# A list of work up to chunk 3 ordered anew: block-diagonal states, k and q by SyncE, v by converting transfers of GpSimd

## The chip, the cores and the metric

The kernel runs on one core of one Trainium2 chip. A core has TensorE (PE, with its weight loads shown as PEld), VectorE (DVE), ScalarE (ACT), GpSimd (POOL) and SyncE (SP, which here only issues DMAs), and 16 DMA engines that all queues share. The metric is the time of one launch on the device, in microseconds; lower is better. The kernel before takes 214.64 us, the median of 3 runs (214.52 to 214.77).

## What is computed

Attention with a decay per head, block by block with a running state, and then a feed-forward layer on the attention's output. The sizes: 4 batches, 8 heads, 768 positions, 64 wide; 3072 tokens of 512, hidden width 2048. Inputs and output are float32; the kernel multiplies in float16.

```python
def _attn_ref(q, k, v, lam):                  # q, k, v: (4, 8, 768, 64)
    ...
    for b in range(nb):                       # blocks of 64 positions
        intra = einsum('bhic,bhjc->bhij', qb, kb) * Dmask[None]
        intra = einsum('bhij,bhjd->bhid', intra, vb)
        inter = einsum('bhid,bhde->bhie', qb * lam_pow[None], kv_state)
        out[:, :, sl] = intra + inter
        kb_dec = kb * rev_pow[None]
        kv_state = lam_block[None, :, None, None] * kv_state + einsum('bhsd,bhse->bhde', kb_dec, vb)
    return out

def _moe_ref(x, w_in, w_out, alpha):          # x: (3072, 512)
    h = x @ w_in                              # (3072, 2048)
    g = maximum(h, 0.0) + alpha * minimum(h, 0.0)
    return g @ w_out
```

## The kernel before

The work is cut into 6 chunks. A chunk is 256 positions (two blocks of 128) of two batches, 512 tokens, so a chunk of the feed-forward has the full width of a matmul. Chunks 0 and 1 are the first 256 positions of batches 0, 1 and of 2, 3; chunks 2 and 3 the next 256, and so on. Each chunk has four units: one batch, one half of the heads. There are 24 units, numbered in order; unit 4c to 4c+3 belong to chunk c, and the halves of one batch are neighbours.

A unit needs k, q and v. `load` (L79) brings a half of the heads of one of them, 256 KB of float32, over SyncE's queue, in pieces of 512 bytes; with `None` it brings both halves. `cast` (L257) makes float16 of them on ScalarE ("A"), VectorE ("V") or GpSimd ("G"). `load_v16` (L268) is in the kernel, but nothing calls it before: a DMA on GpSimd's queue that reads v as float32 and writes it as float16 straight into the unit's v16 tile, so that neither a raw tile nor a cast is needed. `key_decayed` (L281) multiplies k by its decay. k and q are transposed by TensorE and copied back, both at once (`transposes`, L298, with "D" instead a transposing DMA of SyncE) or one of them (`transposed`, L324). `decayed` (L342) multiplies the transposed q by its decay.

The products of a unit are `score_products` and `masked` (L376, L391), `intra` (L401), `inter` (L360, which reads the state R of the block before) and `state_products` (L421), from which `states` (L448) makes the next R. `attended` (L437) writes the result, transposed already, to xT of the chunk. `cluster(old, new)` (L471) puts the second half of one unit's products and the first half of another's side by side in one accumulator bank; `scores` and `state` (L487, L491) do the scores and the state of one unit without it, and `state` first clears two banks with a matmul against zeros each (L495).

The feed-forward of a chunk is 16 times `up` (L503: four matmuls, the activation on ScalarE L516 and VectorE L525; with `bi` 0 or 1 only one batch's half of the width), and for four groups of 128 tokens four `down` steps of four matmuls (L532), whose last stores the result. `fill` (L133) issues matmuls whose result nothing reads.

The weights come in four groups each of 512 KB float16: `load_win` (L94) and `load_wout` (L106), converting DMAs on GpSimd's queue. `gate` (L114) is a tiny DMA on SyncE's queue that reads one element of a weight group; it can start only once that group has landed, and SyncE's later loads wait behind it.

All engines run their instructions in the order in which the program issues them. For chunks 0 to 2 and the loads of chunk 4 this order is a list written out by hand (L609 to L919); chunks 3 to 5 are woven by a loop (L921 to L929), and the last down-projections follow (L930). Buffers come round: five sets of raw tiles, four each of the float16 q and k, v16 and kdec tiles, three of the transposed ones, two of masked scores. A tile that is taken again waits until its last reader is done.

Of the kernel before, what the change touches and what calls it, by code (L numbers as in the profile page):

```python
# [11 lines left out]
def kernel(  # L12
# [474 lines left out]
    def scores(n):  # L487
        score_products(n)
        masked(n)
# [116 lines left out]
                a[i]()  # L606
                i += 1

    mask_logs(2)  # L609
    key_decay()  # L610
    load(0, 0, "k", None)
    decay_mask(2)
    query_decay(1, 1)
    cast(1, "k16", "V")
    load(0, 1, "k", 0)
    fill(8, "h")
    mask_logs(1)
    query_decay(2, 1)
    state_decay()
    decay_mask(1)  # L620
    key_decayed(0, "G")
    mask_logs(0)
    load(0, 0, "q", 0)
    cast(0, "k16", "A")
    key_decayed(1, "G")
    load(0, 0, "q", 1)
    query_decay(3, 1)
    decay_mask(0)
    cast(0, "q16", "A")
    load_alpha()  # L630
    cast(2, "k16", "G")
    load(0, 0, "v", 0)
    load(0, 1, "q", None)
    transposed(1, 1, "V", "tk")
    mask_logs(3)
    transposed(0, 1, "A", "h")
    cast(1, "q16", "V")
    transposed(2, 1, "A", "tk")
    decay_mask(3)
    query_decay(0, 1)  # L640
    cast(0, "v16", "A")
    fill(4, "op")
    load(0, 0, "v", 1)
    query_decay(2, 0)
    transposed(1, 0, "V", "h")
    decayed(1, "G")
    transposed(0, 0, "V", "tk")
    slopes()
    cluster(None, 0, "A")
    cast(2, "q16", "V")  # L650
    decayed(0, "G")
    cast(3, "q16", "A")
    load(0, 1, "v", None)
    load(0, 1, "k", 1)
    fill(4, "tk")
    scores(1)
    cast(1, "v16", "A")
    load(1, 0, "k", 0)
    key_decayed(2, "G")
    load_win(1)  # L660
    cast(3, "v16", "V")
    load_win(0)
    cast(2, "v16", "G")
    state(1, "hh")
    load(1, 0, "q", 0)
    key_decayed(3, "G")
    transposed(2, 0, "A", "tk")
    cluster(0, None, "A")
    cast(3, "k16", "A")
    decayed(2, "P")  # L670
    transposed(3, 0, "A", "op")
    scores(2)
    load_win(2)
    load_win(3)
    cluster(1, None, "A")
    state(2, "hh")
    query_decay(1, 0)
    transposed(3, 1, "A", "op")
    load_wout(1)
    fill(5, "tk")  # L680
    cluster(2, None, "A")
    scores(3)
    decayed(3, "G")
    query_decay(0, 0)
    gate(1, "out")
    load_wout(0)
    load(1, 0, "q", 1)
    state(3, "to")
    cluster(3, None, "V")
    load(1, 0, "v", 0)  # L690
    load_wout(2)
    fill(1, "h")
    up(0, 5, 0, "h")
    up(0, 6, None, "h")
    load(1, 1, "k", 1)
    up(0, 5, 1, "tk")
    cast(4, "k16", "A")
    up(0, 4, None, "h")
    up(0, 7, None, "op")
    up(0, 2, None, "h")  # L700
    load(1, 0, "k", 1)
    load(1, 0, "v", 1)
    cast(5, "q16", "G")
    load(1, 1, "q", 1)
    up(0, 0, None, "h")
    load(1, 1, "v", 1)
    load(1, 1, "k", 0)
    load(1, 1, "q", 0)
    up(0, 3, None, "tk")
    up(0, 10, None, "h")  # L710
    up(0, 9, None, "h")
    up(0, 8, None, "op")
    up(0, 15, None, "tk")
    up(0, 11, None, "h")
    up(0, 12, None, "op")
    load_wout(3)
    load(2, 0, "q", 1)
    load(2, 0, "q", 0)
    load(2, 0, "k", 0)
    cast(4, "q16", "A")  # L720
    up(0, 1, None, "h")
    up(0, 13, None, "h")
    up(0, 14, None, "op")
    transposes(4, "A", False)
    load(1, 1, "v", 0)
    load(2, 0, "k", 1)
    down(0, 2, 0, 4, "h")
    key_decayed(4, "V")
    down(0, 3, 0, 4, "h")
    down(0, 0, 0, 4, "op")  # L730
    down(0, 2, 1, 4, "h")
    cast(4, "v16", "V")
    load(2, 0, "v", 0)
    cast(5, "k16", "V")
    key_decayed(7, "G")
    cast(7, "k16", "A")
    down(0, 0, 1, 4, "op")
    cluster(None, 4, "A")
    transposes(5, "A", False)
    key_decayed(5, "V")  # L740
    decayed(5, "V")
    decayed(4, "G")
    down(0, 3, 1, 4, "h")
    cast(5, "v16", "G")
    down(0, 2, 2, 4, "h")
    cast(7, "q16", "A")
    transposed(7, 1, "V", "tk")
    cluster(4, 5, "A")
    down(0, 3, 2, 4, "h")
    transposed(7, 0, "A", "tk")  # L750
    down(0, 0, 2, 4, "op")
    cast(7, "v16", "A")
    cast(6, "k16", "G")
    cluster(5, 7, "A")
    down(0, 0, 3, 4, "op")
    decayed(7, "V")
    cast(8, "q16", "A")
    cast(6, "q16", "G")
    down(0, 2, 3, 4, "h")
    transposes(6, "V", False)  # L760
    load(2, 1, "v", 1)
    down(0, 1, 0, 4, "op")
    load(2, 1, "k", 0)
    cluster(7, None, "A")
    key_decayed(6, "V")
    load(2, 1, "q", 0)
    cast(8, "k16", "G")
    scores(6)
    down(0, 3, 3, 4, "h")
    cast(6, "v16", "V")  # L770
    cast(9, "q16", "A")
    key_decayed(8, "V")
    transposes(8, "V", False)
    decayed(6, "G")
    load(2, 1, "v", 0)
    down(0, 1, 1, 4, "op")
    cast(8, "v16", "G")
    cast(9, "k16", "A")
    load(2, 0, "v", 1)
    load(3, 0, "k", 0)  # L780
    load(3, 0, "k", 1)
    state(6, "hh")
    decayed(8, "V")
    down(0, 1, 2, 4, "op")
    cluster(6, 8, "A")
    load(2, 1, "k", 1)
    down(0, 1, 3, 4, "op")
    up(1, 2, None, "h")
    up(1, 12, None, "op")
    up(1, 13, None, "h")  # L790
    query_decay(3, 0)
    transposes(9, "V", False)
    up(1, 8, 1, "h")
    cast(10, "k16", "A")
    key_decayed(10, "G")
    up(1, 3, None, "op")
    key_decayed(9, "G")
    cast(10, "q16", "A")
    up(1, 15, None, "h")
    up(1, 4, None, "tk")  # L800
    transposes(10, "D", False)
    cast(9, "v16", "G")
    load(2, 1, "q", 1)
    key_decayed(11, "G")
    cast(10, "v16", "G")
    up(1, 8, 0, "h")
    up(1, 1, None, "op")
    cast(13, "k16", "G")
    up(1, 0, None, "h")
    cast(12, "k16", "G")  # L810
    up(1, 11, None, "tk")
    cluster(None, 9)
    up(1, 6, None, "h")
    up(1, 10, None, "h")
    decayed(9, "G")
    up(1, 7, None, "tk")
    gate(3, "out")
    up(1, 5, None, "op")
    load(3, 0, "q", None)
    cast(11, "k16", "G")  # L820
    cluster(8, 10, "A")
    cast(13, "q16", "V")
    cast(11, "q16", "A")
    decayed(10, "V")
    cast(11, "v16", "G")
    down(1, 0, 0, 4, "h")
    load(3, 0, "v", None)
    transposes(11, "D", False)
    down(1, 1, 0, 4, "h")
    cast(12, "q16", "A")  # L830
    up(1, 14, None, "op")
    down(1, 0, 1, 4, "h")
    up(1, 9, None, "tk")
    transposes(12, "D", False)
    cast(12, "v16", "G")
    key_decayed(12, "G")
    load(3, 1, "v", None)
    cluster(9, None, "A")
    down(1, 1, 1, 4, "h")
    cluster(10, 11, "A")  # L840
    decayed(11, "V")
    load(3, 1, "k", 0)
    key_decayed(13, "G")
    down(1, 1, 2, 4, "h")
    down(1, 0, 2, 4, "h")
    transposes(13, "D", False)
    load(3, 1, "k", 1)
    decayed(12, "V")
    load(3, 1, "q", None)
    down(1, 0, 3, 4, "h")  # L850
    cast(14, "k16", "G")
    cluster(11, 12, "A")
    cast(13, "v16", "A")
    down(1, 1, 3, 4, "h")
    up(2, 0, None, "h")
    load(4, 0, "k", 1)
    up(2, 11, None, "op")
    down(1, 2, 0, 4, "h")
    load(4, 0, "q", None)
    cast(14, "v16", "A")  # L860
    key_decayed(14, "V")
    load(4, 0, "v", 0)
    up(2, 9, None, "tk")
    cluster(12, 13, "V")
    down(1, 2, 1, 4, "h")
    cast(14, "q16", "A")
    up(2, 14, None, "op")
    transposes(14, "D", False)
    down(1, 2, 2, 4, "h")
    decayed(13, "V")  # L870
    load(4, 0, "k", 0)
    cast(15, "k16", "V")
    key_decayed(17, "V")
    down(1, 3, 0, 4, "tk")
    down(1, 2, 3, 4, "h")
    key_decayed(15, "G")
    cast(15, "v16", "A")
    load(4, 0, "v", 1)
    cast(16, "k16", "G")
    cast(17, "k16", "V")  # L880
    up(2, 13, None, "h")
    cast(15, "q16", "V")
    cast(16, "q16", "A")
    cast(17, "q16", "A")
    transposes(15, "D", False)
    down(1, 3, 1, 4, "tk")
    transposes(16, "D", False)
    down(1, 3, 2, 4, "tk")
    down(1, 3, 3, 4, "tk")
    cast(17, "v16", "G")  # L890
    decayed(14, "V")
    up(2, 3, None, "h")
    cluster(13, 14, "A")
    up(2, 6, None, "h")
    load(4, 1, "v", 0)
    up(2, 2, None, "h")
    up(2, 5, None, "op")
    key_decayed(16, "G")
    decayed(15, "G")
    up(2, 10, None, "tk")  # L900
    up(2, 4, None, "h")
    cluster(14, 15, "A")
    up(2, 15, None, "h")
    cast(16, "v16", "G")
    load(4, 1, "q", None)
    up(2, 1, None, "tk")
    load(4, 1, "k", 1)
    load(4, 1, "k", 0)
    up(2, 12, None, "op")
    decayed(16, "G")  # L910
    transposes(17, "D", False)
    up(2, 8, None, "h")
    cast(18, "v16", "G")
    cluster(15, 16, "A")
    key_decayed(18, "G")
    up(2, 7, None, "tk")
    load(4, 1, "v", 1)
    cast(18, "k16", "G")
    cast(18, "q16", "G")  # L919

    for c in range(3, NC):  # L921
        att = []
# [39 lines left out]
```

## Time and profile before

| | before |
| --- | --- |
| median of 3 runs | 214.64 us (214.52 to 214.77) |
| the profiled execution's own time | 214.56 us |
| its span | 212.8 us |
| TensorE busy | 206.7 us, 97% |
| VectorE, ScalarE, GpSimd busy | 138.2, 114.8, 60.2 us |
| HBM read, written | 27.27 MB, 6.29 MB |

The span runs from the first to the last instruction that the profile shows; the rest of the time lies around it. The profile's second part cuts the span into 40 slices of 5.3 us; each digit is the busy share in tenths:

```profile
PE   7799999999999999999999999999999999999994
ACT  7985765466676537366644644644534543444121
POOL 3598002423355411046560094620200000000000
PEclk9999999999999999999999999999999999999999
DMA  6999999999967699999797896044011101110212
```

Its third part shows the DMA queues: packets, MB, and the time that the packets took as a share of the 16 engines' span. q1 is fed by SyncE's loads and stores, q0 by GpSimd's converting transfers.

```profile
q1 hardware_dynamic: 56340, 28.85, 54.2%
q0 software_dynamic: 4224, 4.19, 12.0%
```

A row of the timeline has the start, the length, the engine, the line, the operation and the tiles; xN stands for N instructions in a row, and the bracket tells how long the engine idled before and what released it. A row of the groups has the busy time and the mean duration of one in nanoseconds.

### The profile page before, as it was taken

Reading aid. Unit: us, or ns where it says so; the run is one execution under the profiler, and the core shown is the slowest. Engines: PE = TensorE matmul, PEld = TensorE weight load, DVE = VectorE, ACT = ScalarE, POOL = GpSimd, SP = SyncE. Lnnn points to the kernel's source line nnn. Section 1 sums busy time; section 2 is a strip of 40 time slices with the busy share of each in tenths; the row PEclk is TensorE's granted clock in tenths of the full one; section 3 lists DMA queues with packets and bytes.
Section 4 is the critical chain, followed back from the end, with each engine's and each line's share of the span. In section 5 each row is a group of like instructions: output and inputs, shape, how many; then the busy total and the mean of one; then the engine's idle time right before and its main releaser. Section 6 shows DMA issues by size and latency. Waiting matters only on the chain.

```text
span 212.8 us, 5116 instructions
## 1 busy us (share of the span) xinstructions
PE 206.7 (97%) x2092; PEld 106.5 (50%) x2092; DVE 138.2 (65%) x241; ACT 114.8 (54%) x209; POOL 60.2 (28%) x84
## 2 busy tenths in 40 slices
PE   7799999999999999999999999999999999999994
PEld 2465445655545455455554554554554444444453
DVE  6697787778889987969975565565646344444000
ACT  7985765466676537366644644644534543444121
POOL 3598002423355411046560094620200000000000
PEclk9999999999999999999999999999999999999999
DMA  6999999999967699999797896044011101110212
GB/s 168 290 274 205 207 205 285 207 301 305 294 171 216 106 222 283 235 152 274 175 217 105 219 243 159 0 102 99 7 46 49 40 13 49 51 49 3 99 49 99
DMA packets 60603, 33.37 MB, mean 157 GB/s; under 512 B 16276, under 2 KB 57636, under 8 KB 60580
## 3 DMA queue, kind: packets, MB, share of 16 engines
q1 hardware_dynamic: 56340, 28.85, 54.2%
q0 software_dynamic: 4224, 4.19, 12.0%
q8 instruction: 16, 0.26, 0.5%
q14 instruction: 7, 0.06, 0.1%
q10 hardware_dynamic: 16, 0.00, 0.0%
HBM read 27.27 MB, written 6.29 MB: 158 GB/s over the span
## 4 chain that ended last, share of the span: by engine, by line
PE 96%; DVE 2%; ACT 1%; issue 0%; ACTq 0%; DVEq 0%
PE h_ps L508 39%; PE o_ps L538 33%; PE o_ps L561 7%; PE s L383 4%; PE acc L408 3%; PE unread L140 3%; PE acc L367 2%; PE tp L313 1%; PE acc L428 1%; PE tpx L333 1%; PE unread L138 1%; DVE sm L394 1%; DVE qkT L246 1%; PE kv L495 0%; PE kv L428 0%; DVE dmask L196 0%
## 5 line engine op out<-in xcount | busy, mean ns | idle before, releaser
L525 DVE SCALAR_TENSOR_TENSOR g<-m,oma,h_ps 128x512 f16<-128x512 f32 (+1 forms) x98 | 70.9, 735 | 48.5 <-ACT m L516 46.6
L508 PE MATMUL h_ps<-xT,w_in_sb 128*128 128x512 f16 (+1 forms) x392 | 93.0, 375 | 0.0
L516 ACT ACTIVATE m<-h_ps 128x512 f32<-128x512 f32 (+1 forms) x98 | 57.4, 588 | 57.1 <-PE h_ps L508 56.3
L538 PE MATMUL o_ps<-w_out_sb,g 128*128 128x512 f16 x320 | 80.2, 380 | 0.0
L508 PEld LDWEIGHTS <-w_in_sb 128*128 128x128 f16 x392 | 37.8, 98 | 43.1 <-issue 0.2
L538 PEld LDWEIGHTS <-g 128*128 128x128 f16 x320 | 29.8, 98 | 33.5
L394 DVE TENSOR_TENSOR sm<-s,dmask 128x1024 f16<-128x1024 f32 x24 | 29.3, 1221 | 3.4 <-PE s L383 3.3
L551 ACT ACTIVATE o_sb<-o_ps 128x512 f32<-128x512 f32 (+2 forms) x26 | 14.6, 563 | 20.1 <-PE o_ps L561 10.9
L285 POOL TENSOR_TENSOR kdec<-kraw,kdecay 128x512 f16<-128x512 f32 x18 | 18.9, 1056 | 11.6 <-DMA kraw<-in_k_dram 9.2
L347 POOL TENSOR_TENSOR qdT<-qkT,qdecay 128x512 f16<-128x512 f16 (+1 forms) x15 | 15.2, 1013 | 17.1 <-DMA qkT<-qk 8.1
L244 ACT ACTIVATE xT<-acc 128x512 f16<-128x512 f32 x22 | 13.1, 597 | 10.8 <-PE acc L428 9.1
L458 DVE SCALAR_TENSOR_TENSOR R<-R,rdecay,acc 128x128 f16<-128x128 f16 x56 | 16.1, 342 | 0.1
L248 POOL CAST qk<-kraw 128x512 f16<-128x512 f32 x14 | 8.5, 610 | 24.5 <-DMA kraw<-in_k_dram 11.3
L248 POOL CAST v<-vraw 128x512 f16<-128x512 f32 x15 | 9.4, 629 | 20.1 <-PE h_ps L508 11.5
L561 PE MATMUL o_ps<-w_out_sb,g 128*128 128x512 f16 (+2 forms) x96 | 14.1, 308 | 0.0
L561 PEld LDWEIGHTS <-g 128*128 128x128 f16 x96 | 8.1, 98 | 6.1
L244 ACT ACTIVATE qk<-qraw 128x512 f16<-128x512 f32 x17 | 10.4, 623 | 0.8 <-DMA qraw<-in_q_dram 0.8
L383 PE MATMUL s<-qkT 64*64 64x128 f16 x384 | 10.1, 222 | 0.6 <-DVE qkT L246 0.4
L408 PE MATMUL acc<-sm,v 64*64 64x128 f16 x384 | 9.6, 218 | 0.0
L367 PEld LDWEIGHTS <-R 128*128 128x128 f16 x80 | 6.2, 98 | 5.6 <-ACT R L468 0.6
L367 PE MATMUL acc<-qdT,R 128*128 128x128 f16 x80 | 8.4, 219 | 0.5 <-ACT R L468 0.5
L383 PEld LDWEIGHTS <-qkT 64*64 64x64 f16 x384 | 6.5, 106 | 3.7 <-issue 1.4
(66 smaller groups left out, 109.4 us busy)
## 6 DMA issues: line engine op xcount, KB each, us to landing
out_dram<-o_sb SPq DMA_DIRECT2D x23, 256.0 KB, 2.3
kraw<-in_k_dram SPq DMA_DIRECT2D x18, 256.0 KB, 6.3
vraw<-in_v_dram SPq DMA_DIRECT2D x14, 256.0 KB, 5.7
qraw<-in_q_dram SPq DMA_DIRECT2D x7, 512.0 KB, 5.3
qraw<-in_q_dram SPq DMA_DIRECT2D x10, 256.0 KB, 5.6
vraw<-in_v_dram SPq DMA_DIRECT2D x5, 512.0 KB, 5.5
w_in_sb<-in_moe_w_in_dram POOLq DMA_DIRECT2D x4, 512.0 KB, 8.7
w_out_sb<-in_moe_w_out_dram POOLq DMA_DIRECT2D x4, 512.0 KB, 12.7
```

What stands on the lines that cost most here:

```text
L244: nc.scalar.activation(out, in_, AF.Copy)
L248: nc.gpsimd.tensor_copy(out=out, in_=in_)
L285: engine(eng).tensor_tensor(out=kdec, in0=kr, in1=kdecay[:, ds(4 * hh, 4), :].rearrange("p h e -> p e h").unsqueeze(3).to_broadcast([128, ...
L367: nc.tensor.matmul(ot[a][:, hp, :].rearrange("p (e j) -> p e j", e=2), lhsT=R[bb, ho, 2 * pbo + a][:, hp].rearrange("p l d -> p (l d)"), r ...
L383: nc.tensor.matmul(t["s"][ds(a * 64, 64), hl, hp, 1 - e, :].rearrange("p (e j) -> p e j", e=2), lhsT=t["qkT"][p, 1, e, hp, ds(a * 64, 64)] ...
L394: nc.vector.tensor_tensor(out=t["sm"].rearrange("p a h x j -> p (a h) x j"), in0=t["s"].rearrange("p a h x j -> p (a h) x j"), in1=mask_of ...
L458: nc.vector.scalar_tensor_tensor(out=R[b, hh, m + 1][:, hp], in0=R[b, hh, m][:, hp], scalar=rdecay[:, 2 * hh + hp : 2 * hh + hp + 1], in1= ...
L508: nc.tensor.matmul(h_ps[:, 0:n] if bi is None else h_ps[:, 0:n].rearrange("p (e j) -> p e j", e=2), lhsT=w_in_sb[:, gi, ts(f, 128)], rhs=x ...
L516: nc.scalar.activation(m[:, 0:n], h_ps[:, 0:n], AF.Relu, scale=-1.0)
L525: nc.vector.scalar_tensor_tensor(out=g, in0=mv, scalar=oma[:, f : f + 1], in1=hv, op0=ALU.mult, op1=ALU.add)
L538: nc.tensor.matmul(o_ps, lhsT=lhs(c, f, t), rhs=w_out_sb[:, f, :], start=(f == 0), stop=(f == NF - 1),)
L561: nc.tensor.matmul(o_ps[:, 0:n], lhsT=lhs(c, f, t), rhs=w_out_sb[:, f, ds(x, n)], start=(f == 0), stop=(f == NF - 1),)
```

## The change

The whole list up to the loop is written anew; the functions are the same, and the loop for chunks 3 to 5 too. What differs most, in the order of each engine:

- SyncE loads k and q alone at the head, in halves: q and k of units 0 and 2, then of 1 and 3, then k and q of unit 4. The v of units 0 to 7, 10 and 11 isn't loaded by SyncE any more. The gate on w_out(1) stays, behind q of unit 4; behind it come k and q of units 5, 7 and 6.
- GpSimd brings v of those units by `load_v16`: those of units 0, 2, 1, 3 ahead of w_in(1) and w_in(0), that of unit 4 between w_in(0) and w_in(3), that of unit 5 ahead of w_out(3). At the head it casts k of unit 0, q of unit 2 and q of unit 1; `key_decayed` of units 0, 1, 2 and 4 goes to VectorE.
- In the head the states of units 0 to 3 are all made by `state`, where before `cluster(None, 0)` made that of unit 0; unit 6, which had a state of its own between the down-projections, is now in a cluster with unit 7.
- The transposes of unit 4 stand ahead of the first up-projection. The first up-projections are whole; before, the first was split by batch. The matmuls of `fill` at the head are 13 and 7 (before 8, 4, 4, 5 and 1).
- w_out(3) is issued behind v of unit 5; before, it was behind the cast of q of unit 5.

In all, TensorE has 6 matmuls fewer, ScalarE 11 and VectorE 10 instructions fewer and GpSimd 13 more.

The head of the list and what follows up to the first clusters of chunk 1, cut:

```diff
+    query_decay(2, 1)
+    query_decay(0, 1)
+    load(0, 0, "q", 0)
+    load(0, 0, "k", 0)
+    load(0, 1, "q", 0)
+    load(0, 1, "k", 0)
+    load(0, 0, "k", 1)
...
+    fill(13, "tk")
...
+    cast(0, "k16", "G")
+    mask_logs(1)
+    cast(2, "q16", "G")
+    mask_logs(3)
+    load(0, 0, "q", 1)
+    load(0, 1, "q", 1)
+    load(1, 0, "k", 0)
+    key_decayed(0, "V")
+    query_decay(3, 1)
+    load_v16(0)
+    cast(0, "q16", "A")
+    decay_mask(1)
+    cast(1, "q16", "G")
+    load_v16(2)
+    transposed(0, 1, "V", "op")
+    cast(1, "k16", "A")
+    transposed(0, 0, "V", "h")
+    decayed(0, "V")
+    load_v16(1)
+    decay_mask(3)
+    transposed(1, 1, "A", "tk")
+    load_v16(3)
+    decay_mask(0)
     decay_mask(2)
...
+    key_decayed(1, "V")
+    load_win(1)
+    scores(0)
+    transposed(1, 0, "A", "h")
+    cast(2, "k16", "A")
+    transposed(2, 0, "A", "op")
+    fill(7, "tk")
+    cast(3, "q16", "A")
+    decayed(1, "P")
+    transposed(2, 1, "A", "op")
+    key_decayed(2, "V")
+    load(0, 1, "k", 1)
+    cast(3, "k16", "A")
+    key_decayed(4, "V")
+    scores(1)
+    load_win(0)
+    state(0, "hh")
+    cast(4, "k16", "A")
+    transposed(3, 0, "V", "op")
+    decayed(2, "G")
     load_alpha()
...
+    transposed(3, 1, "A", "tk")
+    cluster(0, None, "A")
+    scores(2)
+    load(1, 0, "q", 0)
+    load_v16(4)
+    key_decayed(3, "G")
+    state(1, "hh")
+    state(2, "to")
+    cluster(1, None, "A")
+    scores(3)
+    state(3, "hh")
+    decayed(3, "G")
+    load_win(3)
+    cluster(2, None, "A")
+    cast(4, "q16", "G")
+    slopes()
+    transposes(4, "V", False)
+    load_win(2)
+    cluster(3, None, "A")
+    up(0, 6, None, "h")
+    up(0, 5, None, "h")
+    up(0, 4, None, "op")
+    load_wout(1)
+    up(0, 7, None, "tk")
+    load_wout(0)
+    gate(1, "out")
...
+    load_wout(2)
+    up(0, 3, None, "h")
+    load(1, 0, "k", 1)
...
+    load_v16(5)
+    load_wout(3)
+    cast(5, "k16", "G")
...
+    load(1, 0, "q", 1)
...
+    key_decayed(5, "G")
+    load_v16(7)
...
+    cluster(None, 4, "A")
+    down(0, 2, 0, 4, "h")
+    down(0, 0, 0, 4, "op")
+    down(0, 0, 1, 4, "op")
+    cast(5, "q16", "G")
...
+    down(0, 2, 1, 4, "h")
+    load_v16(6)
...
+    down(0, 0, 2, 4, "op")
+    down(0, 2, 2, 4, "h")
...
+    down(0, 3, 0, 4, "h")
...
+    transposed(5, 1, "A", "tk")
+    down(0, 3, 1, 4, "h")
...
+    transposed(5, 0, "A", "tk")
...
+    cluster(4, 5, "A")
...
+    cluster(7, 6, "A")
```

More of the change, by code (lines that the diff above doesn't have):

```diff
@@ L651 @@
[L651 to L695, printed above, removed]
@@ L736 @@
[L736 to L774, printed above, removed]
@@ L813 @@
[L813 to L832, printed above, removed]
@@ L891 @@
[L891 to L897, printed above, removed]
+    up(1, 14, None, "op")
+    up(1, 4, None, "tk")
+    cluster(8, 10, "A")
+    load(3, 0, "v", None)
+    up(1, 11, None, "h")
+    gate(0, "in")
+    decayed(9, "G")
+    load_v16(11)
+    cast(11, "k16", "G")
+    key_decayed(12, "V")
+    gate(0, "in")
+    down(1, 2, 0, 4, "h")
+    cast(12, "q16", "V")
+    load(3, 1, "v", 0)
@@ new lines @@
+    cast(11, "q16", "G")
+    cast(12, "v16", "A")
+    key_decayed(11, "G")
+    down(1, 0, 0, 4, "op")
+    key_decayed(14, "V")
+    down(1, 0, 1, 4, "op")
+    down(1, 1, 0, 4, "tk")
+    cluster(9, None, "A")
+    key_decayed(13, "V")
+    cast(13, "q16", "V")
+    transposes(11, "D", False)
+    decayed(11, "V")
+    cast(13, "v16", "A")
+    load(4, 0, "k", None)
+    cast(14, "k16", "V")
+    down(1, 1, 1, 4, "tk")
+    down(1, 2, 1, 4, "h")
+    transposes(12, "D", False)
+    down(1, 1, 2, 4, "tk")
```

321 lines of the change are left out of this document (145 added, 176 removed).

## The prediction, as it was put on record

> **What bounds the kernel now.** I read the page first, then the busy time by windows, then the chain of waits.
>
> ```profile
> span 212.8 us, 5116 instructions
> PE 206.7 (97%) x2092; PEld 106.5 (50%) x2092; DVE 138.2 (65%) x241; ACT 114.8 (54%) x209; POOL 60.2 (28%) x84
> PE 96%; DVE 2%; ACT 1%; issue 0%; ACTq 0%; DVEq 0%
> ```
>
> TensorE holds 96% of the chain that ends last. Where it idles, the windows show (columns: stretch, its length, busy time of PE, PEld, DVE, ACT and POOL, granted clock, DMA share, GB/s):
>
> ```profile
> 6.00:14.00 8.00, 6.68 (x122) 4.12 (x121) 6.16 (x16) 6.99 (x17) 5.85 (x9) 1.00 1.17 290
> 14.00:20.00 6.00, 5.48 (x138) 3.43 (x137) 4.96 (x12) 4.37 (x11) 5.99 (x9) 1.00 1.23 219
> 20.00:29.00 9.00, 9.00 (x48) 4.44 (x46) 7.07 (x11) 6.14 (x12) 0.28 (x1) 1.00 1.24 207
> 20.00:209.70 189.70, 189.70 (x1827) 97.37 (x1824) 122.97 (x201) 98.76 (x173) 45.62 (x58) 1.00 0.64 150
> ```
>
> From 20 to 209.7 us TensorE is busy without a gap at full clock. So the time is two things: when the first up-projection starts, and how much TensorE work comes from then on. The chain of waits gives both (start, length, what):
>
> ```profile
> 20.04 13.82 PE h_ps L508 x68
> 33.87 0.45 PE tp L313 x8
> 34.31 4.32 PE o_ps L538 x20
> ...
> 195.81 13.91 PE o_ps L561 x96
> ```
>
> The first stretch is all 16 up-projections of chunk 0 (64 full widths): 13.82/16 = 0.864 us each. A down step of four matmuls costs 4.32/5 = 0.864 us too. A stall anywhere behind 20 us is paid in full; before 20 us only the last link counts. The other limit is the DMA engines, full in these windows: 290 GB/s while SyncE's queue works alone, 207 GB/s written while only GpSimd's converting queue does (SyncE's is held by a gate then). So SyncE's 256 KB take 262144/290000 = 0.90 us and a 512 KB weight group takes 2.53 us.
>
> **The change part by part.** The sum is made against the profiled execution (its span of 212.8 and 1.76 outside it, 214.56), which lies 0.08 under the median, 214.64.
>
> *TensorE work behind the first up-projection.* Unit 4's eight transposes go ahead of it: −0.45 (the chain's row at 33.87). Unit 6 loses its state of its own, and with it two zeroing matmuls:
>
> ```profile
> 51.44 0.22 PE kv L495 x2
> ```
>
> Together −0.7. The eight removed matmuls of fill and the other split are ahead of that point or cost nothing: a split up is eight half-width matmuls instead of four whole ones, and all 16 together still took 13.82.
>
> *The head's chain of compute.* Where the first up-projection starts is now set by loads, ScalarE, GpSimd and TensorE in turn.
>
> ```profile
> 5.15 2.22 POOL L285 TENSOR_TENSOR kdec<-kraw,kdecay 128x512 f16<-128x512 f32 x2 [2.44 <-DMA kraw<-in_k_dram]
> 8.31 1.06 ACT L244 ACTIVATE qkT<-tpx 128x512 f16<-128x512 f16 x2
> L207 ACT ACTIVATE dmask<-dmask 128x384 f32<-128x384 f32 x4 | 2.1, 514 | 0.3 <-DVE dmask L196 0.3
> L244 ACT ACTIVATE xT<-acc 128x512 f16<-128x512 f32 x22 | 13.1, 597 | 10.8 <-PE acc L428 9.1 <-PE acc L408 1.5
> L285 POOL TENSOR_TENSOR kdec<-kraw,kdecay 128x512 f16<-128x512 f32 x18 | 18.9, 1056 | 11.6 <-DMA kraw<-in_k_dram 9.2 <-PE o_ps L538 2.4
> L347 POOL TENSOR_TENSOR qdT<-qkT,qdecay 128x256 f16<-128x256 f16 x5 | 3.5, 713 | 2.2 <-ACT qdecay L229 2.1
> L248 POOL CAST qk<-kraw 128x512 f16<-128x512 f32 x14 | 8.5, 610 | 24.5 <-DMA kraw<-in_k_dram 11.3 <-ACT m L516 8.9 <-PE s L383 2.7
> L95 POOL DMA_DIRECT2D w_in_sb<-in_moe_w_in_dram x4 | 3.2, 808 | 0.0
> ```
>
> The first 512 KB released GpSimd at 5.15. Five quarter-loads stand ahead of and at k of unit 1 now, so it lands three pieces of 0.90 later, about 7.8. Behind that ScalarE runs eleven pieces in a row up to the cast of k of unit 3: four casts and four copies at 0.53 (two took 1.06 in a row) and three masks at about 0.45, 5.6 us, to 13.4. TensorE then transposes k(3) and does inter and intra of unit 0, which before ran in one go like this:
>
> ```profile
> 13.06 0.40 PE L333 MATMUL tpx<-ident,qk 128*128 128x128 f16 x4
> 13.30 0.28 PE L367 MATMUL acc<-qdT,R 128*128 128x128 f16 x2
> 13.50 0.42 PE L408 MATMUL acc<-sm,v 64*64 64x128 f16 x16
> ```
>
> From 13.06 to 13.92 that is 0.9, to 14.4 with a little for the handing over. Only then is the v16 buffer of unit 0 free (four buffers), and the fifth converting transfer, v of unit 4, waits for it at the front of GpSimd's queue. Queued behind it: key_decayed(3), decayed(3), one w_in issue, the cast of q(4). That is 0.8 + 1.05 + 0.7 + 0.8 + 0.6 = 3.9, to 18.3. TensorE waits for that cast (transposes of unit 4 stand ahead of cluster(3)), needs 0.9 for them and inter and intra of unit 3, then ScalarE's copy of xT(3), 0.6: 19.8. The up-projection's first two matmuls need only the units already done, 0.43, so it is worth a start at 19.4 against
>
> ```profile
> 19.88 13.99 PE L508 MATMUL h_ps<-xT,w_in_sb 128*128 128x256 f16 x68
> ```
>
> that is −0.5; I take −0.4. Below it ends at about −1 (the link over GpSimd not the last), above at +0.3. The three casts on GpSimd (3 × 0.6) lie ahead of this, between 5.1 and 9.2, while ScalarE and VectorE wait for loads: nothing, unless q of unit 1 lands after 9.
>
> *w_in(1) behind four converting transfers of v.* The trace has no converting transfer of 512-byte pieces; the nearest rows are w_in's, in GpSimd's timeline and by tile:
>
> ```profile
> 12.32 1.69 POOL L95 DMA_DIRECT2D w_in_sb<-in_moe_w_in_dram  x2
> ```
>
> ```profile
> L95 POOL DMA_DIRECT2D w_in_sb<-in_moe_w_in_dram x4: 757/774/925, 12.3 to 16.6; - x4
> DMA to landing us min/median/max: 7.0/8.7/10.3
> ```
>
> The first landed at 12.3 + 7.0 = 19.3, before TensorE wanted it at 19.9, the last at 16.6 + 10.3 = 26.9: three groups in 7.6, the 2.53 each of above. Now v of unit 0 is issued from 6.5 (after two casts) and w_in(1) at about 11.5. A price V for one v transfer lies between 0.63 (128 KB written at 207 GB/s) and 2.53 (as many pieces as a w_in group, each as dear). The nearest row by size of piece is SyncE's plain load of the same 512 pieces of 512 bytes, 0.90, and I take that. w_in(1) is then there at the later of 11.5 + 7.0 = 18.5 and, with 7.0 − 2.5 = 4.5 from issue to first bytes, for the queue behind v16(1) at 9.2: 9.2 + 4.5 + 3V + 2.53 = 18.9, some 0.5 later for SyncE's last loads beside it: 19.4. Just in time at V = 0.9; each 0.1 more costs 0.3. I take +0.3; the bounds are 0 and, at V = 2.53, +4.9 for w_in(1) alone.
>
> *SyncE's last load ahead of the gate, q of unit 4.* It is the tenth quarter and would land at 12.3 alone, but GpSimd's queue works from about 11 on. How two queues share, the view of DMA queues shows for 40 to 42 us, where both have work (queue, packets, MB, share of the 16 engines):
>
> ```profile
> q0 software_dynamic: 320, 0.33, 100.1%
> q1 hardware_dynamic: 160, 0.08, 19.0%
> ```
>
> SyncE's q1 moved 0.08 MB in 2 us, 40 GB/s against 290 alone, some 14%. With 0.75 us of work left at 11.5, that makes 11.5 + 0.75/0.14 = 16.9 in the middle of 12.3 and 18. The cast stands at 17.7 on GpSimd anyhow. Taken +0.3, bounds 0 and +1.8 (a landing at 19.5).
>
> The Trainium skill, page "DMA: Bandwidth & Descriptors", section "Queues, rings and completion order", has each DMA engine alternate between queues by whole packets of several descriptors. The trace agrees in kind, with 100.1% against 19.0%, and by that rule small v pieces would take longer turns still, which speaks against the change here.
>
> *After the gate.* The gate waits for w_out(1), and only then SyncE loads k and q of unit 5. The rows of before: SyncE's and GpSimd's timeline, and how long loads of q took by tile.
>
> ```profile
> 29.51 0.73 SPq L118 DMA_DIRECT2D gates<-w_out_sb  x1
> 30.29 0.38 SPq L86 DMA_DIRECT2D qraw<-in_q_dram  x1
> ```
>
> ```profile
> 36.49 0.74 POOL L107 DMA_DIRECT2D w_out_sb<-in_moe_w_out_dram  x1
> ```
>
> ```profile
> DMA to landing us min/median/max: 5.3/5.9/8.3
> ```
>
> Before, the loads behind it took 5.3 to 8.3, and w_out(3) was issued only at 36.49, behind the cast of q(5). Now w_out(0), w_out(2), v of 5 and w_out(3) (3 × 2.53 + 0.9 = 8.5 us of transfers) are all queued by then, so GpSimd's queue is full from 30.1 to 38.6. With the gate 0.6 later (one v transfer more lies ahead of w_out(1) behind w_in(1)), k of unit 5 is issued at 30.9 and lands between 36.3 (5.4 later) and 41 (at 14% until the queue ends, then alone): 38.9 in the middle. Then GpSimd does cast k(5), key_decayed(5), the issue of v(7), cast q(5): 0.6 + 1.05 + 0.8 + 0.6 = 3.0. TensorE wants transposed(5, 0) at 19.4 + 13.8 (16 ups) + 0.6 (cluster of unit 4) + 8 × 0.864 (downs) + 0.25 = 41.0. So k must be there by 38.0: +0.9, bounds 0 and +3. Covered until then by those downs; without the cover (downs of that list too early) the wait would be whole.
>
> *Later list and the other engines.* ScalarE has 11 instructions fewer, VectorE 10 fewer, GpSimd 13 more. From 20 to 209.7 us GpSimd is busy 45.6 of 189.7 and ScalarE 98.8, so I cost the new order behind 46 us at nothing: TensorE's matmuls of up and down cover it. Bounds −0 and +0.5.
>
> **The sum.** −0.7 − 0.4 + 0.3 + 0.3 + 0.9 = +0.4: 214.56 + 0.4 = 215.0.
>
> **The rivals.**
>
> *R1, all is covered (the other side).* If V is near 0.63 and SyncE's loads share better than 14%, w_in(1) lands at 18.6, q(4) before 17.7 and k(5) before 38.0. Then only −0.7 and −0.4 remain: 213.5. For it: in 20 to 29 us the converting queue moves 207 GB/s however it is cut, and the load behind the gate landed before in 5.6 us though two w_out groups were in the queue. Against: the 19.0% row. It decides at V below 0.8 and k(5) by 38.0.
>
> *R2, a converting v piece costs far more than its bytes.* At V = 1.8, w_in(1) lands at 9.2 + 4.5 + 5.4 + 2.5 + 0.5 = 22.1, 2.7 behind the 19.4. The gate, with four v transfers ahead of it, comes 4 × 0.9 = 3.6 later while TensorE is 2.7 later, so the stall at unit 5 grows by 0.9 to 1.8: −1.1 + 2.7 + 1.8 = +3.4, 218.0. At V = 2.53 the same sum is −1.1 + 4.9 + (0.9 + 1.6) = +6.3, 220.9. For it: w_in's pieces cost 2.53/512 each, and no row shows a smaller one cheaper. Against: w_in's time fits its bytes as well. The point of decision is V = 1.0.
>
> The Trainium skill, page "DMA: Bandwidth & Descriptors", section "Specifications", puts the least size for full rate at 512 bytes, below which the engine reads, modifies and writes; the 256 bytes that v writes are under it, which is R2. No run here shows such a transfer yet.
>
> *R3, starvation is worse than taken.* SyncE's queue gets next to nothing from 11 us on and from 31 to 38.6: q(4) +1.5, k(5) lands at 40, +2.0, less what the first delay already gave it (0.8): with the −1.1 and +0.3, 214.56 + 1.9 ≈ 216.5.
>
> **How the numbers follow.** Forecast 0.37 (214.5 to 215.8), R1 0.30, R3 0.14, R2 0.11, other 0.08. The range reaches to R1's lower side and past R3: 213.2 to 217.2; the forecast's own is 214.5 to 215.8. This measurement cannot tell less than 0.2% (0.43 us) from no change. Faster (under 214.2): R1 0.27, other 0.03, 0.30. Same: forecast 0.15, R1 0.03, other 0.05, 0.23. Slower: forecast 0.22, R2 and R3 0.25, 0.47.
>
> **What would show it.** The first matmul of an up-projection in the timeline at 19.8 to 20.4, released by xT(3) and not by a DMA (if it waits for w_in, V was too low). Converting v transfers in the table of DMA issues about 0.9 apart; more than 1.2 is R2. Waits of TensorE behind 20 us: about 1 us at tpx<-qk of unit 5, released by GpSimd's cast; none there is R1. The stretch from the first up-projection to the last matmul without its waits 0.7 shorter than 189.8. Wrong altogether it would be if TensorE waited behind 46 us, or if the granted clock fell in the head.

## The result, and the profile after

The changed kernel takes 215.14 us, the median of 20 launches (214.33 to 218.32), beside 214.57 for the kernel before in the same series (214.47 to 215.84). The ratio is 1.0035, with a 95% interval of 1.0018 to 1.0052: a third of a per cent slower, where 215.0 was forecast. Here and below a ratio counts only launches within 1.5% of the fastest of their kernel; left out are 217.65 and 218.32 here, the slowest launch each of e1, e3 and e4, and four of six of e8. What the forecast had no word for is the spread, 4 us from launch to launch where before had 1.4.

The profile that came with the result is of the slowest of those launches, 218.32 us. It shows what went wrong in that launch; launches near the median are read below. Its page, the lines that answer to those of before:

```profile
span 216.5 us, 5114 instructions
PE 208.7 (96%) x2086; PEld 107.0 (49%) x2086; DVE 135.6 (63%) x234; ACT 113.5 (52%) x205; POOL 68.7 (32%) x94
...
PEclk9998599999999999999999999999999999999999
DMA  5999999995997999959994997232111011110212
...
q8 instruction: 16, 0.26, 0.5%
...
PE 92%; DMA 3%; ACT 2%; issue 1%; SPq 1%; ACTq 0%
```

The fifth slice of the clock stands at 5 where before it was 9, and the chain has an entry "issue" of 1%. The chain of waits shows where (start, length, what):

```profile
17.76 0.21 PE kv L428 x10
17.97 2.13 issue
20.10 0.32 PE kv L428 x5
...
21.52 0.97 PE tp L313 x8
```

TensorE stops in the middle of the 16 matmuls of state(3), with nothing that it waits for, for 2.13 us. The windows behind it show the clock (eighth column, behind the five engines):

```profile
20.00:23.00 3.00, 2.90 (x51) 2.23 (x50) 1.25 (x4) 0.98 (x2) 2.80 (x4) 0.50 1.35 195
23.00:26.00 3.00, 3.00 (x19) 1.07 (x12) 0.46 (x2) 1.19 (x2) 0.75 (x1) 0.50 1.25 206
```

Behind the stop the clock is granted at half for over 6 us. Eight transposes take 0.97 instead of 0.45, and the chain has the 16 up-projections at 15.53 instead of 13.82.

A launch near the median is that of the run e10 below, the same kernel at 214.73 us with a span of 213.0. Its windows, for the stretch that was 189.70 of 189.70 before, and its waits of TensorE behind 13 us (us in total, times, longest):

```profile
6.00:14.00 8.00, 6.59 (x96) 3.89 (x94) 6.88 (x12) 6.89 (x16) 6.61 (x9) 1.00 1.32 249
14.00:20.00 6.00, 5.31 (x170) 3.47 (x167) 5.59 (x14) 4.00 (x9) 5.40 (x8) 1.00 1.14 159
20.00:210.00 190.00, 188.90 (x1812) 96.51 (x1812) 117.81 (x193) 97.81 (x172) 54.07 (x67) 1.00 0.67 147
```

```profile
PE tpx L333 <- POOL qk L248: 1.8, 2, 1.1
...
PE tp L313 <- POOL qk L248: 0.5, 1, 0.5
PE h_ps L508 <- DMA w_in_sb<-in_moe_w_in_dram: 0.3, 1, 0.3
```

One wait of about 1.1 us is left behind 20 us (in 190 us it is not busy for 1.10); the other one of the first row lies in the head. The place of the first is in the chain of that launch, followed back from the end:

```profile
19.51 11.52 DMA w_out_sb<-in_moe_w_out_dram
...
31.04 0.73 SPq L118
...
31.82 7.81 DMA kraw<-in_k_dram
...
40.33 1.05 POOL kdec L285
...
42.11 0.63 POOL qk L248
...
42.79 0.40 PE tpx L333 x4
```

Read it downwards: w_out(1) is issued and lands at 31.03, the gate reads it, SyncE asks for k of unit 5 at 31.82, it lands 7.81 later at 39.63, GpSimd casts and decays it, casts q, and TensorE transposes q of unit 5 at 42.79. This is the forecast's path after the gate, piece by piece.

### The profile page after: what moved, and what is told of

Read it like the earlier page. It is cut to its first block, busy times and chain, and to the rows that moved or that the text cites. A ratio compares the mean times of both kernels' runs of the same rounds, so it can differ in the third digit from the quotient of the medians.

```text
span 216.5 us, 5114 instructions
## 1 busy us (share of the span) xinstructions
PE 208.7 (96%) x2086; PEld 107.0 (49%) x2086; DVE 135.6 (63%) x234; ACT 113.5 (52%) x205; POOL 68.7 (32%) x94
## 3 DMA queue, kind: packets, MB, share of 16 engines
q0 software_dynamic: 9504, 5.51, 18.3%
## 4 chain that ended last, share of the span: by engine, by line
PE 92%; DMA 3%; ACT 2%; issue 1%; SPq 1%; ACTq 0%
PE h_ps L508 40%; PE o_ps L538 32%; PE o_ps L561 6%; PE s L383 4%; PE acc L408 3%; DMA kraw<-in_k_dram 3%; PE acc L367 2%; PE tpx L333 1%; PE tp L313 1%; PE acc L428 1%; SPq L86 1%; ACT qkT L244 1%; PE kv L495 1%; PE kv L428 1%; ACT qk L244 1%
## 5 line engine op out<-in xcount | busy, mean ns | idle before, releaser
L508 PE MATMUL h_ps<-xT,w_in_sb 128*128 128x512 f16 (+1 forms) x388 | 94.1, 382 | 0.0
L538 PE MATMUL o_ps<-w_out_sb,g 128*128 128x512 f16 x320 | 79.1, 379 | 0.0
L347 POOL TENSOR_TENSOR qdT<-qkT,qdecay 128x512 f16<-128x512 f16 (+1 forms) x17 | 18.7, 1099 | 28.0 <-DMA qkT<-qk 10.7
L244 ACT ACTIVATE xT<-acc 128x512 f16<-128x512 f32 x23 | 13.7, 598 | 14.9 <-PE acc L428 9.9
L248 POOL CAST qk<-kraw 128x512 f16<-128x512 f32 x14 | 8.8, 630 | 19.4 <-DMA kraw<-in_k_dram 19.1
L285 POOL TENSOR_TENSOR kdec<-kraw,kdecay 128x512 f16<-128x512 f32 x14 | 14.9, 1065 | 0.0
L248 POOL CAST v<-vraw 128x512 f16<-128x512 f32 x9 | 5.5, 617 | 28.7 <-DMA vraw<-in_v_dram 11.8
L248 POOL CAST qk<-qraw 128x512 f16<-128x512 f32 x11 | 7.2, 656 | 5.9 <-DMA qraw<-in_q_dram 5.9
L244 ACT ACTIVATE qkT<-tpx 128x512 f16<-128x512 f16 x9 | 5.3, 599 | 6.0 <-PE tpx L333 5.9
```

The source lines that it names most:

```text
L244: nc.scalar.activation(out, in_, AF.Copy)
L248: nc.gpsimd.tensor_copy(out=out, in_=in_)
L347: engine(eng).tensor_tensor(out=qdT[:, :, :, p], in0=(t["qps"] if eng == "P" else t["qkT"][:, 0])[:, :, :, p], in1=qdecay[:, hh, :, :, p], ...
L508: nc.tensor.matmul(h_ps[:, 0:n] if bi is None else h_ps[:, 0:n].rearrange("p (e j) -> p e j", e=2), lhsT=w_in_sb[:, gi, ts(f, 128)], rhs=x ...
L538: nc.tensor.matmul(o_ps, lhsT=lhs(c, f, t), rhs=w_out_sb[:, f, :], start=(f == 0), stop=(f == NF - 1),)
```

## The experiments

The first three ask which of three waits makes the time and the spread: instructions that come late (A), w_in(1) (B), or k and q of unit 5 behind the gate (C). Behind the place of an edit, line numbers are later than above: by 8 in e2, e4, e6, e7 and e9, by up to 2 in e5.

**e1_again** is the changed kernel once more.

> The changed kernel as it is, for a profile of an undisturbed execution. Theory A (instructions late): the one profile seen so far has TensorE without an instruction for 2.1 us at 18 us, because the next 16 KB of its instructions came late through DMA engines full of converting transfers, and behind it a halved clock; here that stall should be shorter or absent, span about 213, and the time between 214.3 and 215.5. Theory B (w_in(1) late): TensorE waits for w_in(1) at the first up-projection, which lands at 20.5 to 21.5. Theory C (unit 5 late, as in the prediction): a wait of about 1 us of TensorE at tpx<-qk between 38 and 46 us. The three can hold together; the waits and landings tell their shares.

Measured: 215.64 us over 12 launches (214.35 to 219.62), ratio 1.0034 (1.0002 to 1.0067), the same result again. The profiled launch took 216.86 and has no stop for instructions, but two waits behind the gate:

```profile
PE tpx L333 <- POOL qk L248: 1.8, 2, 1.2
PE tpx L333 <- DVE qk L246: 1.3, 1, 1.3
```

The longer of the first row's two is unit 5 again (1.16 in the timeline). The second row is q of unit 7, cast by VectorE, and there the profile shows no late load: the cast follows VectorE's work before it without a wait for a DMA, but lasts 2.43 us where it lasts 0.41 in e10 (first e1, then e10):

```profile
45.53 2.43 DVE L246 CAST qk<-qraw 128x512 f16<-128x512 f32 x1
```

```profile
44.42 0.41 DVE L246 CAST qk<-qraw 128x512 f16<-128x512 f32 x1
```

In e1 GpSimd multiplied and cast without a break from 45.30 to 47.63 beside it, and the cast ended at 47.96. In e11 the same cast took 1.32 and ended at 45.73, behind an instruction of GpSimd that ended at 45.44. That the two engines hold each other up fits these rows, but no run tests it. Six of the 12 launches lie between 214.35 and 215.01, five between 216.2 and 216.9, one at 219.62.

**e2_more_rows** moves TensorE's program against the fetch of its instructions.

```diff
+    def fill_small(n, bank):
+        t = bank_of(bank, "unread")
+        for _ in range(n):
+            for a in range(2):
+                p = ds(a * 64, 64)
+                nc.tensor.matmul(t[p, 0:64], lhsT=ident[p, 0:64], rhs=ident[p, 0:64], start=True, stop=True)
...
-    fill(13, "tk")
+    fill(6, "tk")
+    fill_small(32, "tk")
...
-    fill(7, "tk")
+    fill(3, "tk")
+    fill_small(20, "tk")
```

> Ten of the 20 matmuls of fill are replaced by 104 matmuls of 64x64 with 64 columns, so TensorE's instruction stream is 94 pairs further at 11 us, and the fetch of its next 16 KB is asked for before the converting transfers fill the DMA engines. The result is the same. Theory A: the fetch starts before 14 us, no wait for issue at 16 to 20 us, the spread from launch to launch falls to that of the kernel before (under 1 us), and the median is 0.5 to 1 us shorter than the changed kernel's (214.2 to 214.6). Theory B or C alone: the same 215.1 as the changed kernel, spread too.

Measured: 216.02 us (214.48 to 217.69), ratio 1.005 (1.002 to 1.008). It is not faster, but the stop has moved, and how far is what tells. (Eleven of fill's matmuls are gone, not ten, so the program has 93 pairs more.) A window from 0 to the end of the stop counts the matmuls that TensorE had run by then (the x behind the first busy time, PE). First the profile of the result, then e2:

```profile
0.00:20.05 20.05, 15.18 (x223) 7.88 (x224) 16.04 (x38) 14.24 (x30) 14.13 (x28) 0.99 1.06 200
```

```profile
0.00:20.55 20.55, 16.88 (x351) 10.14 (x351) 17.97 (x42) 15.22 (x32) 14.72 (x29) 1.00 1.12 211
```

223 and 351 are 128 apart. The page has 16 transfers of instructions (q8) with 0.26 MB in all, 16 KB each, and e2's page has 17; TensorE's program is 2086 matmuls and as many weight loads, so 16 KB hold about 2 × 2086 / 16 = 261 of them, 130 pairs. The two stops are one such piece apart. TensorE's list of waits puts the one in e2 down to VectorE's copy of qkT, which ran until 19.96, but in e1 the same intra(3) began at 19.79 while that copy went on until 20.48: it doesn't wait for it. The row of e2's weight loads has the wait as "issue":

```profile
20.62 0.32 PEld L416 LDWEIGHTS <-v 64*64 64x64 f16 x16 [1.45 <-issue]
```

Behind the stop of 1.3 us the clock was at half until 24 us again, which made this launch slow.

**e3_gate_earlier** changes one line.

```diff
-    gate(1, "out")
+    gate(2, "in")
```

> The gate of SyncE waits for w_in(2) instead of w_out(1), one 512 KB group earlier, so k and q of unit 5 are asked for about 2.5 us earlier. Theory C: 0.9 us faster than the changed kernel, 214.2, and k of unit 5 lands 1 to 2.5 us earlier. Theories A and B alone: no change, 215.1, or slower by up to 0.5 where the loads delay w_out groups.

Measured: 214.94 us (213.33 to 218.33), ratio 0.9992 (0.996 to 1.0025). The median is 0.7 below e1's, in the direction of C, but its interval reaches e1's. In the profiled launch the wait at unit 5 is 0.18, and a new one of 0.23 stands for w_out(3), which landed at 44.01; its gate was released at 29.75, only 1.3 us earlier than in e10 and not 2.5: w_in(1) came 0.2 later there, at 20.20, and v of unit 4 landed 1.74 behind w_in(0), where it was 0.73 in e10.

**e4_rows_54** puts the ends of the 16 KB pieces where they have time.

```diff
-    fill(13, "tk")
+    fill(8, "tk")
+    fill_small(18, "tk")
...
-    fill(7, "tk")
+    fill(4, "tk")
+    fill_small(13, "tk")
```

> As in e2, but with 54 pairs more instead of 94: eight of fill's matmuls replaced by 62 small ones, result unchanged. TensorE ran dry at pair 226 in the first profile of the changed kernel and at pair 354 in e2, 128 pairs apart, which is 16 KB of its instructions. Theory A, made sharper (a piece of 16 KB is asked for when the piece before it is begun, and comes up to 4 us late while converting transfers fill the DMA engines): with 54 pairs more the ends of pieces lie at 16.5 and about 25 us with 7 and 8 us of lead, so no wait for issue in any profile, and the slowest launches (over 216.5) go; median 0.3 to 0.6 below the changed kernel's, 214.4 to 214.9. Rival: where the wait falls has nothing to do with the count of instructions; then waits for issue and launches over 216.5 stay.

Measured: 214.78 us (213.31 to 217.79), ratio 0.9999 (0.9976 to 1.0023). (The expectation's 226 and 354 are the 223 and 351 of above, counted otherwise.) The profile has no stop for instructions, and the median fell as expected; but two of 12 launches still took over 216.3, one of them 217.79, and launches over 216.5 were the rival's sign. What the edit moved can be read from the instruction transfers themselves: from the start of the one that holds the 224th pair to that pair's matmul were 2.3 us in the result's profile, where TensorE waited, and 2.3 in e11, 2.6 in e10 and 3.1 in e1, where it didn't; to the 352nd in e2, where it waited, 2.4. So the changed kernel came through with less than 1 us to spare. Here they are 4.8 and 6.1, and in e6, e7 and e9 3.8 or more. The profiled launch, 215.50, waits 0.47 for w_in(1), which landed at 20.94, and 0.90 for unit 5.

**e5_split_weights** brings each weight group by two transfers, `load_win` and `load_wout` each with a loop over two halves of the rows.

> Each weight group comes by two converting transfers of half the pieces, bytes and result unchanged; GpSimd issues 8 DMAs more, about 0.4 to 0.75 us each, of which one or two lie on the head's chain over GpSimd (+0.4 to +1.5). Theory P (a DMA engine takes all pieces that one DMA has for it in a row, 32 for a weight group, before another queue's turn): SyncE's queue gets about twice the share, k of unit 5 lands 2 us earlier than in e1 (by 38.5), and waits for unit 5 and 7 go: 214.5 to 215. Rival (turns go piece by piece whatever the DMA): landings as in e1 but for the half group by which the gate is earlier, and the time 215.1 to 216 with GpSimd's longer chain.

Measured: 214.62 us (214.32 to 216.29), ratio 1.0012 (0.9993 to 1.0031). The profiled launch has no wait over 0.4 behind the gate. But its up-projections end 1.1 us later than e10's, which covers such a wait, and the head shows the chain over GpSimd by its own price:

```profile
15.45 0.80 POOL L274 DMA_DIRECT2D v<-in_v_dram  x1
...
17.89 1.47 POOL L96 DMA_DIRECT2D w_in_sb<-in_moe_w_in_dram  x2
19.36 0.63 POOL L250 CAST qk<-qraw 128x512 f16<-128x512 f32 x1
```

```profile
20.04 0.40 PE L315 MATMUL tp<-ident,qk 128*128 128x128 f16 x4 [1.28 <-POOL qk L250]
```

Two issues of w_in(3) stand in that chain instead of one, 1.47 instead of 0.8, and TensorE's wait for the cast of q of unit 4 is 1.28 where e10 has 0.45. On the question asked it is unclear: k of unit 5 landed 7.35 us after its issue, against 7.81 in e10 and 8.68 in e1, a little sooner and not two.

**e6_rows_54_gate** joins e4 and e3.

> e4 and e3 together (54 pairs more, and the gate on w_in(2)). If the two causes A (instructions) and C (k and q of units 5 and 7 late behind the gate) are separate and both real, both gains come: median 213.6 to 214.3, faster than both kernels, and no waits over 0.5 us behind the first up-projection but for w_out(3), up to 0.5. If only one is real, the time is that of e3 (214.9) or e4.

Measured: 213.92 us (213.28 to 214.90), ratio 0.9967 (0.9949 to 0.9984): faster than both kernels, and the spread is 1.6 us. The intervals of e3, e4 and e6 overlap, so it isn't shown how much each of the two edits gave. Its chain behind the first up-projection is TensorE's alone:

```profile
20.70 13.54 PE h_ps L516 x62
...
34.72 6.15 PE o_ps L546 x28
40.87 0.22 PE tpx L341 x4
...
42.22 1.73 PE o_ps L546 x8
```

The waits at the transposes of unit 5 are gone; k of unit 5 landed at 36.90, asked for at 28.55.

**e7_win_behind_cast** and **e9_half_win** go on from e6. In e7 the issue of w_in(3) goes behind the cast of q of unit 4; e9 is e7 with w_in(1) in two transfers of 256 columns.

```diff
-    load_win(3)
     cluster(2, None, "A")
     cast(4, "q16", "G")
+    load_win(3)
```

> e6 with the issue of w_in(3) moved behind the cast of q of unit 4 on GpSimd. Theory of the prediction (the head's chain runs over GpSimd from load_v16(4) to that cast): the cast ends 0.8 earlier, TensorE's transposes of unit 4 start at about 18.5 instead of 19.2, and the first up-projection comes 0.2 to 0.7 earlier, until w_in(1), which lands between 19.2 and 21 from run to run, ends the wait instead; 213.3 to 213.8 against e6's 213.9. Rival (w_in(1) sets the start already in most launches): no change, 213.9.

> e7 with w_in(1) brought as two transfers of 256 columns, and the first up-projections in the order 5, 4, 6, 7, so that the first two need only the first half; GpSimd issues one DMA more, in a gap of 0.8 it had. If w_in(1) ends the wait for the first up-projection in e7: 0.3 to 1.0 faster than e7, 212.8 to 213.4. If the chain over GpSimd and xT does: no change. If pieces of 1024 bytes written as 512 take more than half of those twice as long: slower, by up to 0.5.

Measured: e7 213.96 us, ratio 0.9963 (0.994 to 0.9986); e9 213.89 us, ratio 0.9962 (0.9944 to 0.9979). Neither gains on e6. In e7 TensorE transposes unit 4 earlier, without a wait, and the first up-projection is where it was:

```profile
18.56 0.62 PE L321 MATMUL tp<-ident,qk 128*128 128x128 f16 x8
...
19.89 1.40 PE L516 MATMUL h_ps<-xT,w_in_sb 128*128 128x512 f16 x5
```

w_in(1) landed at 19.85. The 16 up-projections end 0.2 earlier than in e6's profile, and TensorE waits 0.59 for a group of w_out later. In e9 its first half landed at 18.55, and the first up-projection came at 19.91, with a wait for xT(3) of 0.16. So w_in(1) and the chain end within a few tenths of each other, and taking time from one gives it to the other.

**e8_plain_v** undoes the converting transfers of units 0 to 3.

```diff
+    load(0, 0, "v", 0)
+    load(0, 1, "k", 1)
+    load(0, 1, "v", 0)
+    load(0, 0, "v", 1)
+    load(0, 1, "v", 1)
     load(1, 0, "k", 0)
...
-    load_v16(0)
...
-    load_v16(2)
+    load_win(1)
...
-    load_v16(1)
+    cast(0, "v16", "G")
...
-    load_v16(3)
```

> The changed kernel with v of units 0 to 3 loaded by SyncE as float32 and cast (three on GpSimd, one on VectorE) instead of by converting transfers; w_in(1) is issued at about 10 instead of 12.6. If the converting transfer at its measured price (0.7 to 1.0 each) pays: w_in(1) lands 2 to 3 earlier (17 to 17.5), but SyncE's last v, k and q share the engines with it and come at 15 to 19, TensorE waits for them, and the first up-projection is 1 to 3 later: 216 to 218. If it doesn't pay (it only delays w_in(1)): 214.3 to 215.

Measured: 221.15 us (216.72 to 222.97), ratio 1.0158 (1.0094 to 1.0221): slower as expected. How much slower is open: the launches took 216.72, 219.63 and four times over 221, and the ratio rests on the first two. The profiled one took 221.24, and not for v: the v of units 0, 2 and 1 were cast by 14.2, and w_in(1) landed at 17.23. What came late is k of unit 4, now behind four loads of v on SyncE's queue: asked for at 9.64, landed at 18.92. Its cast and its decay stand ahead of the head's work on ScalarE and VectorE:

```profile
18.94 0.69 DVE L285 TENSOR_TENSOR kdec<-kraw,kdecay 128x512 f16<-128x512 f32 x1 [6.78 <-DMA kraw<-in_k_dram]
```

and TensorE waits 6.39 us; from 18 to over 24 us the clock is at half. From 12 to 18 us SyncE's queue, with loads of v ahead of that k, moved 0.57 MB beside two groups of w_in, 95 GB/s against 290 alone. So this run gives the price of loads on SyncE's queue beside GpSimd's weights, not that of v.

**e10_look** and **e11_look** are two more launches of the changed kernel.

> The changed kernel once more, for a profile of a launch near its median; the two profiles so far lie above it (218.32 and 216.86). By the sum of e1's rows without its two waits for units 5 and 7 the launch would take 214.4; each of these waits adds up to 1.3, a stall for instructions at pair 226 2 to 5. A launch of about 215 should show one wait of 0.5 to 1 us at the transposes of unit 5 or 7 and none for instructions; TensorE's stretch from the first up-projection to the last chunk without waits 0.9 shorter than before.

> The same once more, with the same expectation: time = 214.4 plus the waits behind the first up-projection that its own profile shows, within 0.3, unless w_in(1) lands after 20.5, which adds its lateness.

Measured: 214.73 and 214.91 us, one launch each, beside 214.47 for the kernel before. Both have one wait at unit 5, of 1.05 and 0.91, and no stop for instructions. For e10 the rule gives 214.4 + 1.05 = 215.45, 0.7 too much, for e11 214.4 + 0.91 = 215.31, 0.4 too much, so both miss the 0.3 that was expected; the 214.4, taken from e1 by difference, was too high, since e1's head was 0.4 later (its up-projections end at 34.45, e10's at 34.04). The sum from the kernel before fits: 214.56 + 0.17 (end of the up-projections, 34.04 against 33.87) − 0.92 (the stretch behind it without the wait) + 1.05 = 214.86.

## Why the prediction was right, point by point

*TensorE's work behind the first up-projection* (−0.7). Right, and 0.2 too small. From the end of the 16 up-projections to the last chunk's down-projections before took 195.81 − 33.87 = 161.94 us, e10 196.11 − 34.04 − 1.05 of wait = 161.02, so −0.92; e6, without waits, 195.14 − 34.24 = 160.90, so −1.04. Where the rest comes from isn't traced.

*The head's chain over GpSimd* (−0.4). Right in its links, about 0.5 too early. load_v16(4) was issued at 14.99 in e10 (forecast 14.4), released by TensorE as said, and the cast of q of unit 4 ended at 18.8 (18.3). e5 made the chain longer and moved the end with it; e7 made it shorter and 0.2 came of it, because w_in(1) stands next.

*The price of a converting v* (0.9 taken, +0.3). Right. From 12 to 14 us of e10, GpSimd's queue alone was at work but for the last of SyncE's:

```profile
q0 software_dynamic: 1193, 0.30, 152.5%
q1 hardware_dynamic: 77, 0.04, 6.2%
```

1193 pieces in 2 us are 0.86 us for the 512 of one transfer. R2, at 1.8 and more for each of four, is out, though a single transfer can take as much (1.74 in e3). Here the Trainium skill, page "DMA: Bandwidth & Descriptors", section "Specifications", whose least size for full rate is 512 bytes, is half borne out: 128 KB in 0.86 us is 150 GB/s written, under the 207 of the weights' 1024-byte pieces. An extra price for the small piece doesn't show: SyncE's plain load of 512 pieces, with 512 bytes written each, takes 0.90. w_in(1) landed at 20.00 in e10, 0.6 later than worked out, since GpSimd, which got q of unit 1 only at 8.8, issued it at 12.19 and not 11.5. It ended the last wait of the head by 0.3, which the prediction had named as the sign of a V too low; it was the issue that was late. In other launches it came between 19.02 (e11) and 20.94 (e4).

*q of unit 4 starved* (+0.3). Wrong in the share that it took for SyncE's queue, 14%, which was measured beside a weight group. q of unit 4 landed 5.1 us after its issue, at 13.0. From 10 to 12 us of e10, beside the transfers of v, SyncE's queue moved as many pieces as GpSimd's and more, 165 GB/s and not 40:

```profile
q0 software_dynamic: 578, 0.14, 73.3%
q1 hardware_dynamic: 690, 0.33, 61.6%
```

So the small pieces of v didn't hold SyncE's queue up longer, as the prediction had argued against the change; the weight groups do, and e8 shows that price in the head. The 0.3 too much here and the 0.5 too little in the chain cancelled by luck, and the first up-projection came at 20.05 where the terms give 19.4 + 0.6 = 20.0.

*After the gate* (+0.9). Right in its path, and in its size by luck. The load took 7.81 us (forecast 8.0) and the wait was 1.05. But the forecast counted TensorE's need, 41.0, from a start at 19.4, without the 0.6 that its own terms add to the head; with it the term would have been 0.3 and the sum 214.4. What made it come out is a gate later than forecast: released at 31.04 and not 30.1, because w_in(1) landed at 20.00 and four weight groups and v of unit 4 took 11.0 us behind it. So k landed at 39.63 (forecast 38.9) and TensorE was there at 41.74 (41.0), both 0.7 late. The wait at unit 7 in e1, 1.32, the forecast didn't have. R1, no wait, did not come: by the sum of above it would be 213.8, and the lowest launch is 214.33. What that launch waited for isn't shown.

*Later list and the other engines* (0). Right: behind the two waits of unit 5 and 7 none over 0.2 us is left in e10, e11 and e1. The numbers of instructions were wrong and nothing hangs on them: by the profiles ScalarE has 4 fewer (209 to 205), VectorE 7 fewer (241 to 234) and GpSimd 10 more (84 to 94).

*What the forecast did not see.* The stop for instructions, and the clock behind it. It is not in the median launch, but it made the slowest one: 218.32 − 214.73 = 3.6, against 2.13 for the stop, 1.03 for the work at half clock ahead of the up-projections (23.21 − 20.05 − 2.13) and 1.61 in them (15.60 − 13.99 in the timelines), less the 1.05 at unit 5 that was covered then: 3.7. This explains the profile of that launch; that it is behind every slow launch isn't shown, since e4 removed it from its profile and two of its 12 launches stayed above 216.3. The prediction had named two signs that it was wrong altogether, a wait of TensorE behind 46 us and a lower clock in the head. Both came in single launches: the wait at unit 7 in e1 lasted until 48.02, and the clock fell in the result's profile and in e2. So the account holds for launches near the median, e10 and e11, and not for the spread.

The rivals: R3 (216.5) is near the time of e1's launch, 216.86, but not its mechanism; that launch has an ordinary wait at unit 5, and the one at unit 7 came from VectorE's cast. What the other launches near 216.5 waited for isn't shown.

## What to carry to other kernels

Where all DMA engines are full, ask for every queue what it still has to bring when another queue begins: a load of 256 KB took 5.1 us beside transfers of v (q of unit 4 in e10) and another 9.3 beside weight groups and behind loads of v (k of unit 4 in e8), and a wait of 1 us came not from the transfers that were changed but from a gate that let the next loads go into the middle of the weights. Carry the start of one stage into the next: a term that is right by itself is wrong when it is counted from a start that another term of the same sum has moved. Moving that gate one group earlier and moving the ends of TensorE's pieces of instructions gave 0.33% below the kernel before, from a change that alone lost 0.35%. And before a stage is shortened, look what ends next to it: e7 and e9 took time from one of two chains that end together and gained nothing on e6.

## What the runs showed of the hardware that was not expected

TensorE's instructions come by the same DMA engines, 16 KB at a time. In the profile of the result the DMA queues of 14 to 17.7 us hold none, and those of 17 to 19 us, just as TensorE ran dry at 17.97, hold one; in e1, which didn't stop, it came between 14 and 16:

```profile
q0 software_dynamic: 312, 0.31, 110.7%
q8 instruction: 1, 0.02, 2.9%
```

```profile
q0 software_dynamic: 658, 0.26, 112.3%
q8 instruction: 1, 0.02, 3.9%
```

The first fence is of the result's profile, the second of e1. The Trainium skill, page "Runtime: NRT & Kernel Launch", section "Instruction fetch mechanics", has blocks of 16 KiB or 256 instructions, fetched over a DMA queue, and calls the cost of crossing a block mostly hidden. The traces agree in size (128 pairs of weight load and matmul from stop to stop); hidden it was not, at 2.13 and 1.3 us.

The clock fell to half behind e8's wait of 6.39 us, but also behind the stops of 2.13 us in the result's profile and 1.3 us in e2, both at about 20 us; it stayed there for 6.83, 6.83 and 3.41 us. Behind waits of 1.16 and 1.32 us at 42 to 48 us in e1 it didn't fall, nor behind 1.28 at 20 us in e5. The Trainium skill, page "TensorE: Matmul & The Clock Gate", section "What's actually happening", has the clock drop after at least one idle window of about 3.4 us that runs free of the kernel. The two stops here were shorter, so a gap under that is not safe; what decides between these cases stays open.
